# The copy of x in 5 KB pieces, a new order for TensorE, and one row multiplication moved on VectorE

## The chip, the cores and the metric

The kernel runs on one core of a Trainium2 chip. The metric is the time of one execution on the device, in microseconds, as the median of several runs. The core has five engines that this kernel drives, each with its own list of instructions: TensorE (PE; its weight loads are shown apart as PEld), VectorE (DVE), ScalarE (ACT), GpSimd (POOL) and SyncE (SP), which here only issues DMAs. ScalarE and GpSimd issue some DMAs too. Sixteen DMA engines carry the transfers.

## The reference

The input x has 2048 rows of 640 values in bf16; the weights are bf16 too. The output is the input plus two branches that read the same layer-normalised rows.

```python
xn = layernorm(x)                              # over 640, eps 1e-5, no gain and no bias
q  = (xn @ wq) -> 32 heads of 20               # k = xn @ wk, v = xn @ wv: one head, shared
p  = softmax(q k^T * 20**-0.5)                 # 32 x 2048 x 2048
A  = concat(p @ v) @ wo                        # 640 x 640
h  = relu(xn @ w1 + b1)                        # 640 x 1536
B  = (h * h) @ w2 + b2
out = x + A + B
```

## The kernel before, in words

**Tiles.** The 32 heads are taken in 8 groups of 4, the 2048 queries in 4 chunks of 512, which makes 32 blocks. Each block runs over 16 key tiles of 128 keys. So a unit of work (block, key tile) is four score tiles, one for each head, of 128 keys by 512 queries. Unit u stands for block u // 16 and key tile u % 16; score tile t belongs to unit t // 4. A score tile is one matmul with 20 rows of contraction into one of eight PSUM banks.

**Two ways to the exponential.** The score tiles are shared out between two engines. ScalarE takes pairs of tiles with its exponential (line 1083; 693 instructions). VectorE takes single tiles or pairs with a trick of its own (line 1093; 656 instructions): a multiply and an add that write 16-bit integers, whose bits are then read as a bf16 power of two. To make that accurate, four versions of the result with shifted exponents are summed; they are called terms 0 to 3. Terms 1 to 3 are made from term 0 by integer additions, on GpSimd (line 1106, and line 1112 for two at a time) or on VectorE (line 1107). To save matmuls, two terms of a unit are often added into one. Such a pair sum is an accumulating DMA that GpSimd issues (line 1130) or an addition on VectorE (line 1128). The terms live in 15 buffers of 128x2048 called tx. TensorE then multiplies the exponentials by v (widened by a column of ones, which gives the softmax sums), into a PSUM bank for each block.

**The written-out order.** Nothing is scheduled at run time and there is no planner in the file: ORDER gives each engine a list of words (lines 67 to 382), and each engine works through its list in order. Which operation needs which others follows from the code; every such dependence on another engine becomes a semaphore wait. TENANTS (line 383) lists who uses each tx buffer in turn. HELD (line 414) makes each of GpSimd's locked operations wait for a named operation of VectorE. The words that matter here:

- `q:40,41@5,6` are the score matmuls of tiles 40 and 41 for ScalarE, into banks 5 and 6; `a:40` is ScalarE's exponential on them. `d:429.1@5` is the score matmul of head 1 of unit 429 for VectorE, and `e:429.1` its VectorE instruction.
- `p:`, `j:` make shifted terms; `s:`, `b:` are pair sums. `u:429.1` are the four matmuls with v of term 1 of unit 429, which may hold a pair sum; `v:422` those of a unit of ScalarE.
- `T13`, `Q1`, `KT6`, `V1`, `FFN1`, `FFN2`, `FP`, `OUT`, `OF` are TensorE's other work: transposes of xn, the projections q, k, v, the feed-forward and the output projection.
- `CM0_2` is a row multiplication on VectorE (line 976): 128 rows of unnormalised head outputs times the broadcast reciprocals of their softmax sums, for query chunk 0 and column block 2. Its inputs come back through DRAM: the sums are stored (SM), laid out for a reciprocal (SL, RC), stored (RS), and broadcast by DMAs on SyncE's queue (OM, BC). Eight of GpSimd's copies (`p:124.3` is the first) are held on CM0_2.

**The start.** The loads of x, `X0` to `X12`, and the weights go mostly over SyncE's queue, in this order: `X0 X2 wq0 X4 X6 X8 b2 X12 xb b1 w11 wq w10 w20`. Some are held by name until an early operation is done (HOLD, line 60). Layer normalisation of row tile st is a statistics step (bn_stats), a reciprocal root `PW` on GpSimd (line 676) and the scaling `XN` on VectorE or GpSimd (line 677); then TensorE transposes (`T`, line 700), and projects. GpSimd's list at the start ends `... PW10 XN10 PW11 XN11 PW12 XA PW13 PW14 XN14 PW15 XN15 LIB` before its first copies.

**The tensor xb.** For the residual the kernel wants x + b2 in row order. xb is a tensor in DRAM of the same size as x, 2048x640 in bf16, 2560 KB. `xb` on SyncE's queue copies x there, DRAM to DRAM (line 647). `XA` on GpSimd's queue is a DMA that adds the broadcast b2 to it in place (line 648); it waits for the copy and for the load of b2. Later, loads `XR` (line 869) fetch 128 rows at a time for the last step of each row tile. `wd0` to `wd3` (lines 641 to 644) are other copies from DRAM to DRAM, of parts of wo. TensorE's list near the arrival of wq is `q:38,39@3,4 q:40,41@5,6 Q1@2 Q1 T12@1 Q1 T13@0 q:42,43@3,4 Q1`; Q1 is the first use of the big load wq.

Of the kernel before, what the change touches and what calls it, by code (L numbers as in the profile page):

```python
# [38 lines left out]
def _pl(z):  # L39
# [455 lines left out]
def bass_parallel_sum__grouped_kv_mqa__dense_activation_squared_relu__prompt_kernel(nc, A_x, A_wq, A_wk, A_wv, A_wo, B_x, B_w1, B_b1, B_w2, B_b2, out):  # L495
    es = ExitStack()
    with es:
# [98 lines left out]
        def load(name, eng, fn, deps=()):  # L596
            return op(name, eng, fn, deps, dma=one())
# [723 lines left out]
```

## Time and profile before

| | |
|---|---|
| median of 3 runs | 663.84 us (662.64 to 665.05) |
| the profiled execution, its own time | 664.51 us |
| its span | 662.7 us |
| mean granted TensorE clock | 1.000 |
| PE / PEld busy | 654.4 / 216.9 us |
| DVE busy | 625.3 us |
| ACT busy | 649.7 us |
| POOL busy | 536.7 us |

The span runs from the first to the last instruction of the profiled execution, and the time lies 1.8 us above it. Busy times are sums of instruction durations on an engine. TensorE's 99% needs care: its matmuls are pipelined and their ends are modelled, so that a TensorE that is kept waiting in short pieces still looks busy; the waits of its weight loads tell more. In a row of the timeline the first number is the start, the second the duration, and the brackets hold the idle time before it and what ended it.

### The profile page before, as it was taken

Reading aid. Unit: us, or ns where it says so; the run is one execution under the profiler, and the core shown is the slowest. Engines: PE = TensorE matmul, PEld = TensorE weight load, DVE = VectorE, ACT = ScalarE, POOL = GpSimd, SP = SyncE. Lnnn points to the kernel's source line nnn. Section 1 sums busy time; section 2 is a strip of 40 time slices with the busy share of each in tenths; the row PEclk is TensorE's granted clock in tenths of the full one; section 3 lists DMA queues with packets and bytes.
Section 4 is the critical chain, followed back from the end, with each engine's and each line's share of the span. In section 5 each row is a group of like instructions: output and inputs, shape, how many; then the busy total and the mean of one; then the engine's idle time right before and its main releaser. Section 6 shows DMA issues by size and latency. Waiting matters only on the chain.

```text
span 662.7 us, 22005 instructions
## 1 busy us (share of the span) xinstructions
PE 654.4 (99%) x9422; PEld 216.9 (33%) x9422; DVE 625.3 (94%) x1123; ACT 649.7 (98%) x716; POOL 536.7 (81%) x532
## 2 busy tenths in 40 slices
PE   8999999999999999999999999999999999999998
PEld 4432222333322223333332222333333322223444
DVE  8879999999999999999999999999999999999997
ACT  7999999999999999999999999999999999999996
POOL 1729899899898889898999989888999988899400
PEclk9999999999999999999999999999999999999999
DMA  8794857888897995696957645798888654858732
GB/s 293 187 245 96 185 110 163 166 183 187 185 186 161 183 182 120 129 184 125 178 107 155 122 92 99 151 189 170 158 174 165 132 121 91 178 105 177 141 110 71
DMA packets 53814, 102.06 MB, mean 154 GB/s; under 512 B 15948, under 2 KB 31452, under 8 KB 53652
## 3 DMA queue, kind: packets, MB, share of 16 engines
q0 software_dynamic: 18544, 68.17, 55.4%
q1 hardware_dynamic: 34308, 31.94, 16.8%
q8 instruction: 74, 1.21, 0.8%
q10 hardware_dynamic: 864, 0.54, 0.3%
q14 instruction: 24, 0.20, 0.1%
HBM read 23.26 MB, written 10.01 MB: 50 GB/s over the span
## 4 chain that ended last, share of the span: by engine, by line
PE 58%; ACT 34%; DMA 3%; DVE 3%; SPq 1%; issue 0%; POOL 0%
PE ps L600 57%; ACT PT L1083 34%; DVE tx L1093 1%; DMA tx<-tx 1%; DMA cmore<-drs 1%; DMA tx<-in_A_x_dram 1%; PE ps L1005 1%; SPq L800 0%; SPq L969 0%; SPq L963 0%; DVE xnT L694 0%; SPq L622 0%; DVE OR L662 0%; PE ps L700 0%; PE ps L703 0%
## 5 line engine op out<-in xcount | busy, mean ns | idle before, releaser
L1083 ACT ACTIVATE PT<-ps 128x1024 bf16<-128x1024 f32 (+1 forms) x693 | 640.4, 1089 | 2.3 <-PE ps L600 1.9
L1093 DVE TENSOR_SCALAR tx<-ps 128x512 uint16<-128x512 f32 x656 | 424.8, 683 | 21.8 <-PE ps L600 15.1
L1106 POOL INT64_ADD tx<-tx x375 | 396.3, 1132 | 54.3 <-DVE big L836 15.2
L600 PE MATMUL ps<-qT,kT 20*128 20x512 bf16 x2048 | 265.4, 384 | 3.3 <-ACT PT L1083 1.2
L600 PEld LDWEIGHTS ps<-qT,kT 20*128 20x128 bf16 x2048 | 69.0, 91 | 248.7 <-ACT PT L1083 132.4
L600 PE MATMUL ps<-PT,vx 128*32 128x512 bf16 x1392 | 131.7, 383 | 0.0
L1130 POOL DMA_DIRECT2D tx<-tx x118 | 121.3, 1028 | 10.3 <-POOL tx L1106 7.8
L600 PE MATMUL ps<-tx,vxs 128*32 128x512 bf16 x1220 | 115.4, 384 | 0.0
L600 PE MATMUL ps<-tx,vx 128*32 128x512 bf16 x864 | 81.3, 384 | 0.5 <-DMA tx<-tx 0.5
L600 PE MATMUL ps<-w_sb,big 128*32 128x320 bf16 x1536 | 79.1, 302 | 0.0
L600 PE MATMUL ps<-xnT,w_sb 128*32 128x512 bf16 x960 | 78.0, 383 | 0.0
L1107 DVE TENSOR_SCALAR tx<-tx 128x2048 uint16<-128x2048 uint16 x89 | 61.2, 700 | 0.6 <-PE ps L600 0.2
L600 PEld LDWEIGHTS ps<-PT,vx 128*32 128x32 bf16 x1392 | 34.6, 95 | 39.1 <-issue 31.1
L600 PEld LDWEIGHTS ps<-w_sb,big 128*32 128x32 bf16 x1536 | 33.8, 95 | 30.2 <-issue 20.0
L600 PEld LDWEIGHTS ps<-tx,vxs 128*32 128x32 bf16 x1220 | 30.0, 94 | 36.1 <-issue 27.1
L828 DVE TENSOR_SCALAR hT_tmp<-ps,b1col 128x512 bf16<-128x512 f32 x48 | 35.7, 744 | 0.8 <-PE ps L600 0.6
L600 PE MATMUL ps<-xnT,wq_sb 128*32 128x512 bf16 (+2 forms) x480 | 35.5, 357 | 0.0
L600 PEld LDWEIGHTS ps<-tx,vx 128*32 128x32 bf16 x864 | 21.4, 94 | 26.2 <-issue 21.5
L600 PEld LDWEIGHTS ps<-xnT,w_sb 128*32 128x32 bf16 x960 | 19.9, 95 | 28.8 <-issue 19.3
L600 PE MATMUL ps<-wo_c,OC 128*32 128x320 bf16 x496 | 28.0, 301 | 0.0
L1112 POOL INT64_ADD tx<-tx x14 | 26.9, 1924 | 0.9 <-DVE big L836 0.5
L944 DVE COPY OR<-ps 128x512 f32<-128x512 f32 x30 | 20.4, 680 | 1.7 <-PE ps L600 1.6
(87 smaller groups left out, 221.5 us busy)
## 6 DMA issues: line engine op xcount, KB each, us to landing
tx<-tx POOLq DMA_DIRECT2D x111, 512.0 KB, 5.9
tx<-tx POOLq DMA_DIRECT2D x7, 1024.0 KB, 8.8
w_sb<-in_B_w_dram SPq DMA_DIRECT2D x8, 480.0 KB, 9.6
big<-OR SPq DMA_DIRECT2D x71, 40.0 KB
xb<-in_A_x_dram SPq DMA_DIRECT2D x1, 2560.0 KB, 11.1
xb<-b2r POOLq DMA_DIRECT2D x1, 2560.0 KB, 19.8
xr<-xb SPq DMA_DIRECT2D x16, 160.0 KB, 3.2
out_dram<-out_sb SPq DMA_DIRECT2D x14, 160.0 KB, 3.6
```

Source lines behind the costliest of these rows:

```text
L600: return lambda e: e.matmul(out_(), l, val(r), start=val(start), stop=val(stop), tile_position=tp, skip_group_check=loose)
L828: o = evac(ref, f"RL{qc}_{f}", "DVE", lambda e: e.tensor_scalar(out=hT_tmp[:, k % 2, :], in0=ps[:, ref.n, :], scalar1=b1col[:, f:f + 1], s ...
L944: tn = evac(pv_ref[b], f"TN{b}", "DVE", lambda e: e.tensor_copy(out=OR[:, a, :], in_=acc()), or_users[a])
L1005: parts = [lambda e, l=l, r=r, first=first, last=last: e.matmul(ps[:, at(ref), 0:HW], l, r, start=first, stop=last, skip_group_check=k < N ...
L1083: o = op(f"a:{a}", e, lambda e, qk=qk, slots=slots: e.activation(out=some(PT, slots), in_=some(ps, [r.n for r in qk.takes]), func=AF.Exp, ...
L1093: o = op(f"e:{a}", e, lambda e, x=x, i=i, n=n, refs=refs: e.tensor_scalar(out=x.ref(0)[:, i * 512:(i + n) * 512].bitcast(U16) if n == 1 el ...
L1106: fn = dict(POOL=lambda e, x=x, j=j: e.int64_add(out=x.ref(j).bitcast(I64), in0=x.ref(0).bitcast(I64), in1=TSTEP * j * 0x0001000100010001) ...
L1107: DVE=lambda e, x=x, j=j: e.tensor_scalar(out=x.ref(j).bitcast(U16), in0=x.ref(0).bitcast(U16), scalar1=TSTEP * j, scalar2=None, op0=ALU.a ...
L1112: o = op(f"j:{w}", e, lambda e, x=x: e.int64_add(out=two(*sorted((x.at[2], x.at[3]))).bitcast(I64), in0=two(*sorted((x.at[0], x.at[1]))).b ...
L1130: fn = (lambda e, x=x: e.dma_start(*reversed(sums_of(x.at)), accum_op=ALU.add)) if k == "b" else (lambda e, x=x, p=pairs[0]: e.dma_start(x ...
```

## The change

There are three edits.

First, the copy of x to xb. Before, both sides were read as 128 places of 16 rows each (20 KB in one piece), which is contiguous over the whole tensor. Now the 16 rows of each place are cut into four pieces of 4 rows (5 KB), and the pattern goes over the four pieces outermost, then over the 128 places. The same bytes go to the same addresses.

Second, TensorE's list is written anew. It holds the same 3,184 words. 1,146 of them stand at another position, by at most 27 entries; the first difference is entry 260. 247 of the bank numbers differ. Among the words that move are 18 uses of pair sums (`u:429.1`, `u:95.1`, `u:124.3` and others), which stand later.

Third, in VectorE's list CM0_2 moves behind four other entries. The lists of ScalarE, GpSimd and SyncE, TENANTS and HELD are as before.

```diff
 # TensorE's list, near 160 us
-        "q:468,469@0,1 d:143.2@5 u:125.3 v:112 u:127.2 q:470,471@2,3 d:142.0@5 d:143.3@6 d:142.2@4 q:472,473@0,1 u:124.3 u:126.3 u:124.2 d:142.1@5 q:474,475@2,3 v:116 q:476,477@0,1 "
+        "d:143.1@6 u:126.2 d:143.2@5 d:123.3@4 q:468,469@0,1 u:125.3 v:112 u:126.3 u:127.2 q:470,471@2,3 d:142.0@6 u:127.1 q:472,473@0,1 d:142.2@4 d:143.3@5 u:125.2 v:116 q:474,475@2,3 "
...
 # TensorE's list, near 546 us
-        "u:429.3 q:1690,1691@0,1 d:446.1@5 u:428.1 u:429.1 d:446.2@6 q:1692,1693@2,3 v:421 v:419 u:428.2 d:445.1@5 q:1694,1695@0,1 d:445.0@4 u:427.3 u:426.3 u:426.0 q:1696,1697@2,3 "
+        "u:429.3 u:427.3 u:426.0 q:1692,1693@2,3 d:446.2@5 v:421 d:445.0@6 q:1694,1695@0,1 d:445.1@4 u:426.3 u:428.1 d:446.3@5 q:1696,1697@2,3 u:429.1 v:422 FFN2_3@4 d:444.0@6 "
...
 # VectorE's list
-        "e:126.3 e:126.1 p:127.2@8 e:125.3 e:125.0 e:124.2@13 e:125.1 QCe1_1 p:125.1@7 e:124.0 e:124.1 p:126.3@0 e:123.0@4 TN6 FE29 e:123.1 e:124.3 CM0_2 e:143.0@1 e:123.2 FE30 e:143.1 "
+        "e:126.3 e:126.1 p:127.2@8 e:125.3 e:125.0 e:124.2@13 e:125.1 QCe1_1 p:125.1@7 e:124.0 e:124.1 p:126.3@0 e:123.0@4 TN6 FE29 e:123.1 e:124.3 e:143.0@1 e:123.2 FE30 e:143.1 CM0_2 "
...
-        l_xb = load("xb", "SP", lambda e: e.dma_start(xb.rearrange("(p a) d -> p (a d)", p=128), A_x[0].rearrange("(p a) d -> p (a d)", p=128)), [HOLD["wq"]])
+        l_xb = load("xb", "SP", lambda e: e.dma_start(xb.rearrange("(p g a) d -> g p (a d)", p=128, g=4), A_x[0].rearrange("(p g a) d -> g p (a d)", p=128, g=4)), [HOLD["wq"]])
```

305 rows, old and new, of the table ORDER are left out of this document.

## The prediction, made before the result was known

> **What bounds the kernel now.** I read the page's busy shares first, then the costliest group of ScalarE, then the list of waits (total us, count, us each).
>
> ```profile
> span 662.7 us, 22005 instructions
> PE 654.4 (99%) x9422; PEld 216.9 (33%) x9422; DVE 625.3 (94%) x1123; ACT 649.7 (98%) x716; POOL 536.7 (81%) x532
> ...
> L1083 ACT ACTIVATE PT<-ps 128x1024 bf16<-128x1024 f32 (+1 forms) x693 | 640.4, 1089 | 2.3 <-PE ps L600 1.9
> ```
>
> ```profile
> PEld ps L600 <- ACT PT L1083: 134.5, 355, 0.7
> ...
> DVE OC L976 <- DMA cmore<-drs: 1.1, 1, 1.1
> ...
> PEld ps L600 <- DMA tx<-tx: 0.8, 1, 0.8
> ```
>
> PE's 99% is no work bound: 355 times its weight loads waited for ScalarE to give back a score bank. ScalarE is the bound. Its 693 exponentials fill 640.4 us and it idled 2.3 us before them; neither their number nor their order changes. So the time is the start, 640 us of exponentials, the exponentials' idle time, and a tail. An idle microsecond of ScalarE is a microsecond of the kernel, and no later work gives it back. ScalarE's timeline after the first 29 us shows where such idle time is (start, length, and in brackets the idle time before it):
>
> ```profile
> 29.39 131.64 ACT L1083 ACTIVATE PT<-ps 128x1024 bf16<-128x1024 f32 x143
> 161.23 9.28 ACT L1083 ACTIVATE PT<-ps 128x1024 bf16<-128x1024 f32 x10 [0.20 <-PE ps L600]
> 171.29 329.50 ACT L1083 ACTIVATE PT<-ps 128x1024 bf16<-128x1024 f32 x358 [0.79 <-PE ps L600]
> 500.98 45.94 ACT L1083 ACTIVATE PT<-ps 128x1024 bf16<-128x1024 f32 x50 [0.19 <-PE ps L600]
> 547.18 69.36 ACT L1083 ACTIVATE PT<-ps 128x1024 bf16<-128x1024 f32 x75 [0.26 <-PE ps L600]
> 616.72 37.72 ACT L1083 ACTIVATE PT<-ps 128x1024 bf16<-128x1024 f32 x41 [0.18 <-PE ps L600]
> ```
>
> **The change, part one: what the new orders can win.** The five gaps sum to 0.20+0.79+0.19+0.26+0.18 = 1.62 us; that is all that a better order of PE or VectorE can take from idle time of this size. Two have a cause that the change touches. The 0.26 us at 547 follow PE's 0.8 us wait for a pair sum (its DMA, tx<-tx), which the list of waits shows once; the new order takes u:429.1 twelve entries later. The 0.79 us at 171 follow VectorE's wait for a broadcast row:
>
> ```profile
> 166.15 1.30 DVE L1093 TENSOR_SCALAR tx<-ps 128x512 uint16<-128x512 f32 x2
> 168.51 0.69 DVE L976 TENSOR_TENSOR OC<-cmore 128x512 bf16<-128x512 f32 x1 [1.05 <-DMA cmore<-drs]
> 169.12 1.28 DVE L1093 TENSOR_SCALAR tx<-ps 128x512 uint16<-128x512 f32 x2
> 170.32 0.48 DVE L890 TENSOR_TENSOR OC<-ps,xr 128x320 f32<-128x320 f32 x1
> ```
>
> ```profile
> 169.39 3.06 POOL L1106 INT64_ADD tx<-tx  x3 [1.90 <-PE ps L600]
> ```
>
> The multiplication at 168.51 is CM0_2. It moves behind three of the 0.6 us instructions (two start in 1.28 us) and the 0.48 us one, so it would start near 167.4+3×0.6+0.45 = 169.7, a microsecond after its row landed. The wait goes. What is late next is GpSimd: eight of its copies are held on CM0_2 by name, the first three being the x3 at 169.39, which start 0.2 us after CM0_2 ends. They would start near 170.5, 1.1 us later. That delay is hidden only if the pair sums behind these copies have as much to spare; if not, PE pays up to 1.1 us there. The rest of PE's order (1,146 of 3,184 entries at other places, by at most 27, the first near 67 us) keeps the same matmuls, and its switches between score groups and other work go from 1,302 to 1,300, so its work costs nothing more. A nearby reordering can also make gaps like the 0.2 us ones. Bounds: 1.6 us won, 1.1 us lost. I take 0.8 us won: both named gaps (1.05 us) less a little for GpSimd.
>
> **Part two: the copy of x.** Its pattern was 16 rows for each of 128 places, contiguous over the whole tensor. Now its outermost count is g = 4, then 128, then 5 KB. What this does to the spread over the DMA engines is the question. [...]
>
> ```profile
> xb<-in_A_x_dram SPq DMA_DIRECT2D x1, 2560.0 KB, 11.1
> xb<-b2r POOLq DMA_DIRECT2D x1, 2560.0 KB, 19.8
> ...
> tx<-in_A_x_dram SPq DMA_DIRECT2D x2, 160.0 KB, 3.1
> ...
> wod<-in_A_wo_dram SPq DMA_DIRECT2D x1, 120.0 KB, 2.4
> ...
> wod<-in_A_wo_dram SPq DMA_DIRECT2D x1, 100.0 KB
> ...
> wod<-in_A_wo_dram SPq DMA_DIRECT2D x1, 60.0 KB
> ```
>
> The three last go from DRAM to DRAM on SyncE's queue, as the copy does. The one with 96 outer rows has a landing time; the two whose outermost count is 4 (4×20 rows and 4×12 rows, the same form as 4×128 pieces) have none. [...] I take it that each outer row goes to one engine, which is four engines; the other end is sixteen, as now. [...]
>
> How fast one engine goes follows from two stretches inside the copy (the last two columns are the mean busy share of 16 engines and GB/s):
>
> ```profile
> 11.00:12.00 1.00, 1.00 (x47) 0.74 (x47) 1.00 (x5) 1.00 (x3) 0.00 (x0) 1.00 1.76 586
> 13.00:14.00 1.00, 0.57 (x7) 0.24 (x6) 1.00 (x5) 0.74 (x2) 0.53 (x1) 1.00 1.55 614
> ```
>
> 614/(1.55×16) = 24.8 GB/s, and 586/(1.76×16) = 20.8 GB/s, for each busy engine. Four engines carry 2,621,440/4 = 655,360 bytes each: 26.4 us at 24.8, 31.5 us at 20.8. The fixed part of a transfer is about 2.7 us (the 160 KB load: 3.1 us less 10 KB/24.8). So landing takes 29.1 to 34.2 us in place of 11.1. I take 29.1, for four engines are less crowded than sixteen. Issuing 512 pieces costs SyncE what a 640-piece load costs, 0.64 us against 0.50, which nobody waits for. Who waits for the landing:
>
> ```profile
> 9.80 0.50 SPq L647 DMA_DIRECT2D xb<-in_A_x_dram  x1
> ...
> 19.09 0.60 SPq L630 DMA_DIRECT2D w_sb<-in_B_w_dram  x1
> ...
> 19.73 0.64 SPq L628 DMA_DIRECT2D wq_sb<-in_A_wq_dram  x1
> ...
> 25.96 1.82 POOL L648 DMA_DIRECT2D xb<-b2r  x1
> 27.99 0.56 POOL L676 TENSOR_TENSOR rstd<-mv,nhalf 128x1 f32<-128x1 f32 x1 [0.21 <-DVE mv L667]
> ...
> 29.00 0.75 DVE L677 TENSOR_SCALAR big<-tx,mv,rstd 128x640 bf16<-128x640 bf16 x2
> 29.29 0.61 PE L600 MATMUL ps<-xnT,wq_sb 128*20 128x512 bf16 x8
> ...
> 30.56 0.47 PE L700 MATMUL ps<-ident,big 128*128 128x128 bf16 x5
> ```
>
> The copy is issued at 9.80 and landed at 20.9; with four engines it lands at 38.9 (44.0 at the slower rate). First gate: GpSimd's accumulating DMA XA (25.96) waits for it, and GpSimd works in order, so queued behind it are PW13, PW14, XN14, PW15 and XN15, and behind those VectorE's XN13 and PE's T13 (30.56). From XA to T13 the least is 1.82+0.21+0.56, then half of the 0.75 us pair and two releases, about 3.4 us: T13 at 42.3, 11.7 us late. Second gate: wq (19.73) and the w1 load ahead of it (19.09) are queued behind the copy on SyncE's queue:
>
> ```profile
> w_sb<-in_B_w_dram SPq DMA_DIRECT2D x2, 480.0 KB, 5.9
> wq_sb<-in_A_wq_dram SPq DMA_DIRECT2D x1, 700.0 KB, 5.7
> ```
>
> If each engine takes them in order, the four busy ones have still 480/16 = 30 KB and 700/16 = 44 KB to move, 3 us at 24.8 GB/s: wq at 41.9, where Q1 on PE needs it at 29.29, 12.6 us late. Either gate stops PE, whose order puts every further score group behind Q1 and T13. The shift is the later of the two, not their sum; I take 12.2 us, between them. Bounds: 11 us below, 17 us above (44.0+3 for wq). Cover is missing: from 29.39 ScalarE runs without a gap, so it holds no stock of scores and loses the same 12 us.
>
> After an idle stretch PE may also be slow. Two rows of the same shape, early in the kernel and at its very start (busy us, mean ns of one, idle before):
>
> ```profile
> L1041 PE MATMUL ps<-hT_tmp,OR 128*128 128x512 bf16 x15 | 5.2, 508 | 0.0
> ...
> L710 PE MATMUL ps<-hT_tmp,OR 128*128 128x512 bf16 x3 | 1.5, 626 | 1.3 <-DVE PT L608 1.3
> ```
>
> The page's row of the granted clock has 9 in all slices:
>
> ```profile
> PEclk9999999999999999999999999999999999999999
> ```
>
> The slow matmuls stand at the very start, and whether a pause in mid-kernel would bring them back no row here shows; the sum has none. [...]
>
> The copy's other followers are covered: XA's own 19.8 us would end at 38.9+19.8 = 58.7, and its first reader starts at 53.0 now, which moves to 65.
>
> ```profile
> L869 SPq DMA_DIRECT2D xr<-xb x16: 328/478/1443, 53.0 to 527.5; - x16
> ```
>
> **Sum.** 12.2 - 0.8 = 11.4 us. On the profiled execution (664.51 us, span 662.7 and 1.8 us around it) that is 675.9; this execution lies 0.67 us above the median of the runs, 663.84. Forecast: 675.3.
>
> **Rivals.** *The copy stays hidden.* Its price is 0 if it lands by XA's 25.96, that is within 16.2 us of issue. At 24.8 GB/s that takes 8 engines or more (320 KB each, 13.2+2.7 = 15.9 us). It would be so if the pieces were spread, or joined again to the whole contiguous tensor, in which case the edit does nothing. For it: all pieces together are contiguous, as now. Against it: the blank rows with outer count 4. Then only 0.8 us is left: 663.84-0.8 = 663.0, no change that can be measured; with all 1.62 us and the small gaps won, 661.5, faster.
>
> *GpSimd late behind CM0_2, and no copy trouble*: the 1.1 us of its held copies reach PE, and the reordering makes one or two new gaps of the 0.8 us kind: 663.84+1.1+1.0 = 665.9, barely slower. For it: the 1.90 us idle before 169.39 ended with CM0_2. Against: 1.1 us is all it can be.
>
> *Only one gate, or a half one*: wq overtakes the copy on the twelve free engines and the four others finish early, so that only XA's chain counts and part of it is caught up because GpSimd's normalisations run back to back: 669 to 672. For it: of the 0.75 us pairs that VectorE does between those steps some could run ahead of the landing. Against: T13 alone is enough for 11 us.
>
> **How the numbers follow.** Four engines, both gates or the later one: 0.72, 671 to 683. Half gate: 0.09. Hidden copy: 0.16, of which 0.05 faster and 0.11 within. GpSimd late: 0.03, slower by a hair in half of it. A measurement of this kernel can tell about 0.3%, 2 us, from no change. So slower 0.82, same 0.13, faster 0.05. The likeliest case has 671 to 683 as its own range, worked from 11 and 17 us and the clock's unknown; to hold eight in ten I go down to the half gate's 668 and up to 683.
>
> **What would show it.** The copy's landing near 29 us instead of 11.1, or none printed; packets of 5 KB; XA near 39; a hole of ScalarE from about 31 to 43 us; and after it the same 640 us of exponentials, without the gaps at 171 and 547. A landing time near 11 us for the copy would make the prediction wrong at its root; a late landing with no hole in ScalarE would make it wrong at the gates.

## The result: 681.27 us, and the profile after

The changed kernel takes 681.27 us (median of 5 runs, 679.44 to 681.83), the kernel before beside it 663.99 us (662.64 to 665.05). The ratio is 1.0255, with a 95% interval of 1.0235 to 1.0276: slower by 17.3 us. The profiled execution took 681.83 us with a span of 680.0 us. Medians of the same kernel before in later comparisons were 663.4 to 664.2 us; each experiment is held against the one it ran beside. Single executions of one kernel can be some us longer at a lower granted clock: of 23 of the kernel before, 18 have a clock of 1.000 and take 662.3 to 664.2 us, and five have 0.992 to 0.997 and take 664.6 to 668.9 us.

From the page after, the busy shares, the granted clock, the chain that ended last and ScalarE's group (line numbers are one lower than before):

```profile
PE 659.6 (97%) x9422; PEld 217.7 (32%) x9422; DVE 626.9 (92%) x1123; ACT 650.4 (96%) x716; POOL 535.8 (79%) x532
...
PEclk9959999999999999999999999999999999999999
...
PE ps L599 64%; ACT PT L1082 26%; DMA xb<-in_A_x_dram 4%; PE ps L1004 1%; DVE tx L1092 1%; POOL tx L1105 0%; PE ps L699 0%; DVE tx L1106 0%; POOL xb L647 0%; ACT xnT L695 0%; DVE OR L661 0%; DVE tx L1127 0%; DVE OR L662 0%; DVE ident L612 0%; DVE PT L610 0%
...
L1082 ACT ACTIVATE PT<-ps 128x1024 bf16<-128x1024 f32 (+1 forms) x693 | 641.1, 1086 | 18.6 <-PE ps L599 18.2
```

The busy time of the exponentials is 641.1 us against 640.4, but the idle time ahead of them went from 2.3 to 18.6 us. These 16.3 us and the 0.7 us are 17.0 of the 17.3 us by which the spans differ. The copy of x now stands in the chain with 4% of the span, some 27 us; before it was not in it. And the granted clock has a slice of 5 tenths. ScalarE's timeline shows where the idle time is:

```profile
14.39 17.44 ACT L1082 ACTIVATE PT<-ps 128x1024 bf16<-128x1024 f32 x17 [0.27 <-PE ps L599]
44.68 2.10 ACT L1082 ACTIVATE PT<-ps 128x1024 bf16<-128x1024 f32 x2 [12.84 <-PE ps L599]
47.90 1.02 ACT L1082 ACTIVATE PT<-ps 128x1024 bf16<-128x1024 f32 x1 [1.11 <-PE ps L599]
49.41 1.94 ACT L1082 ACTIVATE PT<-ps 128x1024 bf16<-128x1024 f32 x2 [0.49 <-PE ps L599]
51.70 1.94 ACT L1082 ACTIVATE PT<-ps 128x1024 bf16<-128x1024 f32 x2 [0.35 <-PE ps L599]
54.61 121.48 ACT L1082 ACTIVATE PT<-ps 128x1024 bf16<-128x1024 f32 x132 [0.98 <-PE ps L599]
...
192.02 5.61 ACT L1082 ACTIVATE PT<-ps 128x1024 bf16<-128x1024 f32 x6 [0.41 <-PE ps L599]
198.20 1.02 ACT L1082 ACTIVATE PT<-ps 128x1024 bf16<-128x1024 f32 x1 [0.57 <-PE ps L599]
199.82 319.11 ACT L1082 ACTIVATE PT<-ps 128x1024 bf16<-128x1024 f32 x347 [0.60 <-PE ps L599]
```

There are three things to explain: a hole of 12.84 us from 31.8 to 44.7 us, four gaps of together 2.93 us right behind it, and three gaps of 1.58 us at 192 to 200 us. The hole first, on the engines that the prediction named (SyncE, GpSimd, TensorE), and the DMA view's rows for the big transfers:

```profile
9.77 0.73 SPq L646 DMA_DIRECT2D xb<-in_A_x_dram  x1
16.57 5.43 SPq L630 DMA_DIRECT2D b1row<-in_B_b_dram  x1
...
22.71 7.00 SPq L627 DMA_DIRECT2D wq_sb<-in_A_wq_dram  x1
...
38.02 1.82 POOL L647 DMA_DIRECT2D xb<-b2r  x1 [11.54 <-DMA xb<-in_A_x_dram]
...
41.20 1.04 PE L599 MATMUL ps<-xnT,wq_sb 128*20 128x512 bf16 x8 [11.34 <-DVE mv L669]
```

```profile
xb<-in_A_x_dram SPq DMA_DIRECT2D x1, 2560.0 KB
...
wq_sb<-in_A_wq_dram SPq DMA_DIRECT2D x1, 700.0 KB, 18.4
```

The copy no longer has a landing time, like the outer-count-4 copies before. GpSimd waited 11.54 us for it and issued XA at 38.02, so it landed about 28.2 us after its issue at 9.77. The load wq, issued at 22.71, took 18.4 us in place of 5.7 and landed at 41.1; TensorE's first use of it, Q1, starts at 41.20 after 11.34 us of idling. (The row names a VectorE instruction as the releaser; an experiment below, where that one is early, names the load.) Behind the hole TensorE is slow. From its stretches (us, then busy time of PE, PEld, DVE, ACT, POOL, then the granted clock):

```profile
28.00:30.00 2.00, 1.86 (x48) 0.89 (x36) 1.83 (x8) 2.00 (x4) 0.00 (x0) 1.00 0.26 108
30.00:34.00 4.00, 0.00 (x0) 0.00 (x0) 0.00 (x0) 1.83 (x2) 0.00 (x0) 0.88 0.73 241
34.00:38.00 4.00, 0.00 (x0) 0.00 (x0) 0.00 (x0) 0.00 (x0) 0.00 (x0) 0.50 0.58 191
...
50.00:52.00 2.00, 2.00 (x26) 0.81 (x27) 0.98 (x2) 1.65 (x3) 0.00 (x0) 0.50 1.06 222
...
53.00:54.00 1.00, 1.00 (x28) 0.69 (x24) 0.56 (x3) 0.64 (x1) 0.00 (x0) 0.75 1.10 243
```

The clock fell to a half at about 33.0 us (0.88 over 30 to 34 is 0.96 us at a half), 3.2 us after TensorE's last matmul at 29.9, and came back at about 53.5 us.

### The profile page after: what moved, and what is told of

It is laid out like the page before. It is cut to its first block, busy times and chain, and to the rows that moved or that the text cites. A ratio compares the mean times of both kernels' runs of the same rounds, so it can differ in the third digit from the quotient of the medians.

```text
span 680.0 us, 22015 instructions
## 1 busy us (share of the span) xinstructions
PE 659.6 (97%) x9422; PEld 217.7 (32%) x9422; DVE 626.9 (92%) x1123; ACT 650.4 (96%) x716; POOL 535.8 (79%) x532
## 3 DMA queue, kind: packets, MB, share of 16 engines
q1 hardware_dynamic: 34744, 31.94, 16.3%
## 4 chain that ended last, share of the span: by engine, by line
PE 66%; ACT 26%; DMA 4%; DVE 2%; POOL 1%; issue 0%
PE ps L599 64%; ACT PT L1082 26%; DMA xb<-in_A_x_dram 4%; PE ps L1004 1%; DVE tx L1092 1%; POOL tx L1105 0%; PE ps L699 0%; DVE tx L1106 0%; POOL xb L647 0%; ACT xnT L695 0%; DVE OR L661 0%; DVE tx L1127 0%; DVE OR L662 0%; DVE ident L612 0%; DVE PT L610 0%
## 5 line engine op out<-in xcount | busy, mean ns | idle before, releaser
L1082 ACT ACTIVATE PT<-ps 128x1024 bf16<-128x1024 f32 (+1 forms) x693 | 641.1, 1086 | 18.6 <-PE ps L599 18.2
L599 PE MATMUL ps<-tx,vxs 128*32 128x512 bf16 x1220 | 113.1, 384 | 1.1 <-POOL tx L1105 1.1
L1106 DVE TENSOR_SCALAR tx<-tx 128x2048 uint16<-128x2048 uint16 x89 | 63.1, 721 | 0.3
L599 PE MATMUL ps<-xnT,wq_sb 128*32 128x512 bf16 (+2 forms) x480 | 35.9, 368 | 11.9 <-DVE mv L669 11.3
L599 PEld LDWEIGHTS ps<-w_sb,big 128*32 128x32 bf16 x1536 | 33.8, 95 | 30.3 <-issue 20.4
L599 PEld LDWEIGHTS ps<-tx,vx 128*32 128x32 bf16 x864 | 21.4, 95 | 25.3 <-issue 21.1
L943 DVE COPY OR<-ps 128x512 f32<-128x512 f32 x30 | 20.5, 682 | 2.1 <-PE ps L599 1.9
```

The lines of the kernel that those rows point to most:

```text
L599: return lambda e: e.matmul(out_(), l, val(r), start=val(start), stop=val(stop), tile_position=tp, skip_group_check=loose)
L943: tn = evac(pv_ref[b], f"TN{b}", "DVE", lambda e: e.tensor_copy(out=OR[:, a, :], in_=acc()), or_users[a])
L1082: o = op(f"a:{a}", e, lambda e, qk=qk, slots=slots: e.activation(out=some(PT, slots), in_=some(ps, [r.n for r in qk.takes]), func=AF.Exp, ...
L1106: DVE=lambda e, x=x, j=j: e.tensor_scalar(out=x.ref(j).bitcast(U16), in0=x.ref(0).bitcast(U16), scalar1=TSTEP * j, scalar2=None, op0=ALU.a ...
```

## The experiments

**The parts, each alone.** The copy alone; both orders with the old copy; CM0_2 alone; TensorE's order alone.

```diff
 a1_copy_only: the kernel before, with
-xb.rearrange("(p a) d -> p (a d)", p=128)            # and the same for x
+xb.rearrange("(p g a) d -> g p (a d)", p=128, g=4)
 a2_orders_only: the changed kernel, with these two lines the other way
 a3_row_mult_only: the kernel before, with
-e:123.1 e:124.3 CM0_2 e:143.0@1 e:123.2 FE30 e:143.1
+e:123.1 e:124.3 e:143.0@1 e:123.2 FE30 e:143.1 CM0_2
 a4_tensore_only: the kernel before, with the new list of TensorE
```

> The kernel before with only the new pattern of the copy of x. My theory: the whole loss is the late landing of the copy. The trace after shows ScalarE idle for 12.84 us at 31.8 and for 1.11, 0.49, 0.35 and 0.98 us up to 54.6, in all 15.8 us; all of these should be here, and the copy should land about 28 us after its issue at 9.8. Time 663.99+15.8 = 679.8 us (678.5 to 681.3). Rival: the new orders share in the loss (the gaps of 1.58 us at 192 to 200 in the trace after are theirs, and perhaps some of those at the start); then this kernel keeps below 678.5.

> The changed kernel with the old pattern of the copy, so only the new orders of TensorE and VectorE. By the prediction: both named gaps (0.79 and 0.26 us) are gone and nothing is lost, 663.99-0.8 = 663.2 us. Rival, GpSimd late behind CM0_2: its held copies start late, TensorE waits for terms (0.38 and 0.67 us as in the trace after), ScalarE gets gaps of 0.41, 0.57 and 0.60 us near 176 to 184; then 663.99-1.05+1.58 = 664.5 us. No hole at the start by either.

> The kernel before with only CM0_2 moved behind four entries on VectorE. By the prediction VectorE's wait of 1.05 us and ScalarE's gap of 0.79 us go, and GpSimd's eight held copies start about 1.1 us later without harm: 663.2 us. Rival: the late copies reach TensorE as waits for terms made by GpSimd, 0.4 to 0.7 us each, and the time is 664 to 665 us.

> The kernel before with only TensorE's new order. By the prediction the gap of 0.26 us at 547 goes with the wait for the pair sum, the gap of 0.79 us at 171 stays: 663.7 us. Rival: the new order makes new gaps of the 0.2 us kind, as many as it takes: 664.0 us, and with a loss of its own near 180 us, 665 us.

| kernel | us, median | beside the kernel before |
|---|---|---|
| copy alone | 678.79 (678.09 to 680.48) | 663.53, ratio 1.0233 (1.0211 to 1.0256) |
| both orders | 665.11 | ratio 1.0030 (1.0004 to 1.0056) |
| CM0_2 alone | 669.31 (665.8 in two runs, 669.3 to 671.7 in four) | ratio 1.0077 (1.0047 to 1.0107) |
| TensorE's order alone | 663.36 | ratio 1.0009 (0.9982 to 1.0035) |

The copy makes 678.79-663.53 = 15.3 us and the orders 665.11-663.53 = 1.6 us, together 16.8 of the 17.3. With the copy alone, ScalarE's gaps behind 31 us are these:

```profile
44.59 2.10 ACT L1083 ACTIVATE PT<-ps 128x1024 bf16<-128x1024 f32 x2 [13.23 <-PE ps L600]
47.81 1.02 ACT L1083 ACTIVATE PT<-ps 128x1024 bf16<-128x1024 f32 x1 [1.12 <-PE ps L600]
49.32 3.93 ACT L1083 ACTIVATE PT<-ps 128x1024 bf16<-128x1024 f32 x4 [0.49 <-PE ps L600]
53.47 123.14 ACT L1083 ACTIVATE PT<-ps 128x1024 bf16<-128x1024 f32 x134 [0.22 <-PE ps L600]
176.80 338.46 ACT L1083 ACTIVATE PT<-ps 128x1024 bf16<-128x1024 f32 x368 [0.20 <-PE ps L600]
515.45 114.91 ACT L1083 ACTIVATE PT<-ps 128x1024 bf16<-128x1024 f32 x125 [0.19 <-PE ps L600]
```

Its time lies in the range of my theory (678.5 to 681.3), 1 us below its middle; but that the copy is the whole loss does not hold, for the orders cost 1.6 us beside it. Something unforeseen is in the last two rows. After 176.80 there is no gap like the 0.79 us of before, though CM0_2 stands at its old place. And the 125 exponentials from 515.45 run through the place of the 0.26 us gap (547 us before), though TensorE's list is the old one. VectorE's rows of that multiplication, with the old place of CM0_2, in four kernels (copy alone, TensorE's order alone, and the two copies of the next set, which change nothing at this place):

```profile
182.95 0.68 DVE L976 TENSOR_TENSOR OC<-cmore 128x512 bf16<-128x512 f32 x1
```

```profile
167.31 0.68 DVE L975 TENSOR_TENSOR OC<-cmore 128x512 bf16<-128x512 f32 x1
```

```profile
169.36 0.69 DVE L976 TENSOR_TENSOR OC<-cmore 128x512 bf16<-128x512 f32 x1 [1.27 <-DMA cmore<-drs]
```

```profile
167.51 0.69 DVE L976 TENSOR_TENSOR OC<-cmore 128x512 bf16<-128x512 f32 x1 [0.43 <-DMA cmore<-drs]
```

The wait for the broadcast row was 1.05 us in the execution that I read, and 0, 0, 1.27 and 0.43 us in these. ScalarE's gap behind it was 0.79 us there, and none, none, 1.01 and 0.17 us here, so it follows the wait. Each kernel was profiled once, so that the wait varies between executions of one kernel is inferred from five kernels that do the same at this place; the 0.79 us were no fixed gain in any case, and neither were the 0.26. What the move costs is seen better. With CM0_2 alone moved, GpSimd, TensorE and ScalarE show:

```profile
175.54 3.05 POOL L1106 INT64_ADD tx<-tx  x3 [3.39 <-DVE OC L976]
...
178.65 0.40 PE L600 MATMUL ps<-tx,vxs 128*32 128x512 bf16 x4 [1.02 <-POOL tx L1106]
...
179.45 7.44 ACT L1083 ACTIVATE PT<-ps 128x1024 bf16<-128x1024 f32 x8 [1.24 <-PE ps L600]
```

GpSimd idles 3.39 us for CM0_2 (1.90 before, and 0.75 with the copy alone, where the row was there in time), TensorE then waits 1.02 us for a term that GpSimd made, and ScalarE loses 1.24 us. So the rival, GpSimd late, holds, and it costs more than I gave it: 2.3 us by the two runs at 665.8 (against 663.53), of which ScalarE's rows show 1.24 us here and 0.33 us at 187. The four other runs have a further loss, and a granted clock of 0.987 to 0.995 where the two have 1.000. In the profiled one of them (669.33 us) the granted clock's row has a slice of 7 tenths, from 16.7 to 33.4 us, its mean of 0.995 over the 667.5 us of the span makes some 6.7 us at a half, and ScalarE has three gaps of 1.92, 0.20 and 1.42 us between 14 and 24 us; without these 3.54 us it would be 665.8 too. Why so many of this kernel's runs have it stays open; two runs of the kernel before, of 23, were as long (668.48 and 668.87). TensorE's new order by itself changes nothing that can be measured; together with the move it takes back some 0.7 us of the 2.3 (by the two runs at 665.8). The rest is the gaps of 0.41, 0.57 and 0.60 us in the changed kernel; with both orders and the old copy the same three are there, 0.40, 0.57 and 0.60 us. Both waits for GpSimd's terms stand in the trace after:

```profile
188.15 3.05 POOL L1105 INT64_ADD tx<-tx  x3 [3.37 <-DVE OC L975]
...
191.26 0.40 PE L599 MATMUL ps<-tx,vxs 128*32 128x512 bf16 x4 [0.38 <-POOL tx L1105]
...
197.08 0.40 PE L599 MATMUL ps<-tx,vxs 128*32 128x512 bf16 x4 [0.67 <-POOL tx L1105]
```

**The same pieces, larger counts.** The pieces stay 512 of 5 KB; only the outermost count of the pattern changes.

```diff
 the kernel before, with
-xb.rearrange("(p a) d -> p (a d)", p=128)            # and the same for x
+xb.rearrange("(p g a) d -> g p (a d)", p=64, g=8)    # b1_outer8
+xb.rearrange("(p g a) d -> g p (a d)", p=32, g=16)   # b2_outer16
```

> The kernel before with the copy in the same 5 KB pieces, but with 8 as the outermost count and 64 places. My theory: each outer row goes to one DMA engine, so 8 engines carry 320 KB each, 13.2 us at 24.8 GB/s and 2.7 us around it: landing about 16 us after issue, near GpSimd's 25.96, and wq a little late behind it. Loss 0 to 2 us, 664 to 666. Rival: 5 KB pieces themselves are slow and the count of engines does not matter: landing near 28 us and about 680 us.

> The kernel before with the copy in the same 5 KB pieces, but with 16 as the outermost count and 32 places. My theory: 16 engines carry it, it lands within 11 to 12 us as before, and the time is 664.0 us (663 to 665). Rival: small pieces from DRAM to DRAM are slow by themselves: landing near 28 us and about 680 us.

The first took 664.66 us, the second 663.72, the kernel before beside them 664.15; neither is apart from it (the ratio's interval is 0.9948 to 1.0024 and 0.9938 to 1.0025). With 8, GpSimd's row says when the copy had landed, and TensorE's next row what was left of the second gate; with 16 the DMA view has a landing time again:

```profile
26.90 1.82 POOL L648 DMA_DIRECT2D xb<-b2r  x1 [1.50 <-DMA xb<-in_A_x_dram]
...
29.92 0.61 PE L600 MATMUL ps<-xnT,wq_sb 128*20 128x512 bf16 x8 [1.14 <-DVE mv L667]
```

```profile
xb<-in_A_x_dram SPq DMA_DIRECT2D x1, 2560.0 KB, 11.9
```

Landing takes 28.2 us with 4, 26.90-9.77 = 17.1 us with 8, and 11.9 us with 16. The rival that pieces of 5 KB are slow by themselves is dead. I had assumed that each outer row goes to one DMA engine. By it 4 and 8 engines with 26.4 and 13.2 us of bytes at 24.8 GB/s differ by 13.2 us, and measured they differ by 11.1. With 16 the same sum would be 6.6+2.7 = 9.3 us; 11.9 are measured, near the 11.1 of the old pattern, so with 16 the rate that was read for four is not kept. The traces' records of single packets show it: the copy's 512 packets of 5 KB were on the mean 3.9 at a time under way with a count of 4, 7.5 with 8 and 12.9 with 16, each at 25.5, 24.3 and 20.1 GB/s. (The old pattern went as 64 packets of 40 KB, 14.5 at a time, each at 21.4 GB/s.) The traces' landing records go the same way: the copy before has sixteen, the changed kernel's copy has five, one at 10.90 us and four at 37.06 to 37.70, and of the sixteen of wq behind it twelve stand at 33.1 to 33.8 us and four at 40.4 to 41.1. That fits a copy that kept four of sixteen engines busy; no record names an engine.

**The two gates apart.** The copy keeps its outer count of 4. XA goes behind the normalisations on GpSimd, or wq goes ahead of the copy on SyncE's queue, or both.

```diff
 a1_copy_only, with
-PW12 XA PW13 PW14 XN14 PW15 XN15 LIB       # GpSimd
+PW12 PW13 PW14 XN14 PW15 XN15 XA LIB       # c1_add_late, c3_both
+PW12 PW13 PW14 XN14 PW15 XN15 LIB XA       # c5_both_lib_first
-X12 xb b1 w11 wq w10                       # SyncE
+X12 wq xb b1 w11 w10                       # c2_wq_ahead, c3_both, c5_both_lib_first
```

> Only the new copy, and GpSimd's accumulating DMA XA moved behind XN15, so that no normalisation waits for the copy. If XA on GpSimd is the gate, the hole goes: 664 to 667 us. If wq, queued behind the copy, is the gate, the hole of 12.8 us stays whole, since Q1 waits until 41.1: 679 to 680 us. Both gates are within 0.2 us of each other in the trace after (XA's chain lets T13 go near 41.2, wq lands near 41.1), so I expect the second.

> Only the new copy, and the load wq issued ahead of it on SyncE's queue. If wq is the only gate, the hole goes: 664 to 667 us. If XA on GpSimd is a gate of its own, T13 waits until about 42 and the hole stays: 679 to 681 us, which I expect.

> Only the new copy, with both moves: XA behind XN15 on GpSimd, and wq ahead of the copy on SyncE's queue. By the theory of two gates the hole goes, although the copy still lands near 38 us and XA near 57 us: 664 to 666 us. If something else waits for the copy (b1 behind it on the queue, the loads XR from 53 us on), a hole of 2 us or more stays.

With XA late the time is 680.62 us, with wq ahead 678.80; each gate alone keeps the whole hole (12.47 and 13.66 us of ScalarE, against 13.23 with the copy alone). TensorE's rows at the end of the hole, first with XA late, then with wq ahead:

```profile
41.37 1.03 PE L600 MATMUL ps<-xnT,wq_sb 128*20 128x512 bf16 x8 [10.97 <-DMA wq_sb<-in_A_wq_dram]
```

```profile
40.20 1.82 POOL L648 DMA_DIRECT2D xb<-b2r  x1 [14.73 <-DMA xb<-in_A_x_dram]
...
43.18 0.73 PE L700 MATMUL ps<-ident,big 128*128 128x128 bf16 x5 [13.05 <-DVE mv L667]
```

In the first the load itself is named: TensorE idles 10.97 us for wq. In the second wq is long there (it landed 4.9 us after its issue), and TensorE waits 13.05 us for the transpose's normalised rows, 3 us behind XA. With both moved, the hole of 31 to 45 us is gone, as expected, but the time is 677.55 us (673.23 to 688.78) where 664 to 666 were expected: a new wait came, which I had not foreseen. From GpSimd, TensorE and ScalarE of that kernel:

```profile
40.27 1.82 POOL L648 DMA_DIRECT2D xb<-b2r  x1 [7.13 <-DMA xb<-in_A_x_dram]
51.50 4.08 POOL L1106 INT64_ADD tx<-tx  x4 [9.41 <-issue]
...
53.60 0.62 PE L600 MATMUL ps<-tx,vxs 128*32 128x512 bf16 x4 [4.47 <-POOL tx L1106]
...
14.12 36.07 ACT L1083 ACTIVATE PT<-ps 128x1024 bf16<-128x1024 f32 x37 [0.65 <-PE ps L600]
55.26 1.02 ACT L1083 ACTIVATE PT<-ps 128x1024 bf16<-128x1024 f32 x1 [5.07 <-PE ps L600]
```

ScalarE runs 36 us through the place of the hole. But XA stood ahead of GpSimd's library load LIB. Its 9.41 us began only after XA, the first copies came at 51.50, and TensorE ran out of terms. From 50.9 to 85.0 us the granted clock stood at a half, and in that stretch ScalarE has 17 more gaps, 10.4 us together. So the move was made once more, with XA behind LIB.

> As the kernel with both moves, but XA now stands behind LIB, GpSimd's library load, whose 9.41 us without an instruction were what delayed the first copies there (51.50 after XA at 40.27). With wq ahead of the copy and XA behind LIB, the copy may land near 40 us and nobody should wait for it but XA: GpSimd's first copy starts near 42, no hole of ScalarE at 31 to 45, no lowered clock, 664 us (663.3 to 666). If a third follower of the copy exists, a gap of more than 1 us stays and names it.

```profile
11.60 43.57 ACT L1083 ACTIVATE PT<-ps 128x2048 bf16<-128x2048 f32 x44
58.43 1.02 ACT L1083 ACTIVATE PT<-ps 128x1024 bf16<-128x1024 f32 x1 [3.26 <-PE ps L600]
...
41.80 1.81 POOL L648 DMA_DIRECT2D xb<-b2r  x1 [9.40 <-issue]
...
57.73 0.61 PE L600 MATMUL ps<-qT,kT 20*128 20x512 bf16 x4 [3.41 <-DMA qT<-QCr]
```

The 44 exponentials from 11.60 to 55.17 have no gap, with the copy's count still 4: the two gates are all that the hole was made of. The time is not settled by that. The 12 runs lie between 664.88 us (granted clock 1.000) and 687.63 us, with a median of 673.63, where 663.3 to 666 were expected. The profile shown is of one of the three longest (685.66 us, clock 0.968), and in it a third follower appears: TensorE waits 3.41 us for a small load of the projected queries (qT<-QCr), while XA's 2560 KB and the weights that came late are under way. That these crowd the small load out was not tried. In the execution shown the clock then stood at a half from about 57.2 to 101.6 us (0.86 over 50 to 60, 0.50 from 60 to 100, 0.92 over 100 to 110). What the other runs lose no profile shows.

**The clock.** TensorE is kept busy through its wait by matmuls on zeros.

```diff
 a1_copy_only, with
-q:40,41@5,6 Q1@2 Q1 T12@1
+q:40,41@5,6 fill ... fill Q1@2 Q1 T12@1    # 26 fills in c4_fill, 53 in c6_fill_full
```

> Only the new copy, with 26 groups of matmuls on zeros put on TensorE ahead of Q1, which add nothing to the result and keep TensorE busy for about 10 of the 11.3 us that it waits. By the theory that a lowered clock makes the gaps of 1.11, 0.49, 0.35 and 0.98 us after the hole, the granted clock stays at 1.00, these gaps go, and the time is 2.9 us (2 to 3.3) below the kernel with the new copy alone, near 677 us. Rival: the gaps come from late work on GpSimd and VectorE, and stay: 680 us.

> Only the new copy, with 53 groups of matmuls on zeros ahead of Q1 (26 of them took 5.79 us and left TensorE idle for 6.76 us, and the clock still fell to a half at 39.7). 53 take 11.8 us, so TensorE is hardly idle. By the theory that the lowered clock makes the gaps behind the hole (1.12, 0.49 and 0.22 us with the copy alone), the clock stays at 1.00 and the time is 1.8 us lower than with the copy alone: near 677.0 us. Rival: the gaps are late work of other engines and stay: 678.8 us. The hole itself, about 13 us, stays by both.

The 26 groups of four took only 5.79 us: the row holds 104 matmuls that overlap, for one on zeros is listed with 389 ns in the trace before. TensorE still idled 6.76 us, the clock fell to a half (0.87 over 38 to 40 us, 0.50 from 40 to 48), and the time was 679.24 us: nothing was won, and the test said nothing. With 53 the clock stays up and the time is 674.96 us (674.49 to 675.43), 3.8 us below the copy alone. From its page and ScalarE's timeline:

```profile
PEclk9999999999999999999999999999999999999999
```

```profile
44.09 129.64 ACT L1083 ACTIVATE PT<-ps 128x1024 bf16<-128x1024 f32 x141 [12.87 <-PE ps L600]
```

The hole is there (12.87 us), and the gaps behind it are not: 141 exponentials run through. So the gaps were the clock's, not late work of other engines. The saving is twice the 1.8 us that I had read off the listed gaps. The two profiled executions differ by less than the medians, 678.09-675.43 = 2.7 us, of which 1.8 us are the gaps and 0.4 us the hole (13.23 to 12.87). The other 0.5 us, and the 1.1 us by which the medians differ more, no row shows.

## Why the prediction was right, and where it was not

The forecast was 675.3 us, in a range of 668 to 683; measured are 681.27. The direction and the cause were right, and the loss was 17.3 us where 11.4 were forecast. The bounds of the two terms alone (17 us lost, 0.8 won) would end at 680.0 us; it is the allowance for the clock's unknown in the range that takes in 681.27.

*The bound.* Right: the exponentials' 641.1 us and the tail stayed, and the whole loss is ScalarE's idle time (16.3 us of it in the group's row).

*Four engines.* Right, as far as the records tell. The blank landing times of the outer-count-4 copies were the sign (in the trace before, each of the two has five landing records and the one of 96 rows has sixteen), and with counts of 4, 8 and 16 the copy landed 28.2, 17.1 and 11.9 us after its issue. Landing 28.2 us, 29.1 were forecast. That each outer row goes to one engine was an assumption; no run shows an engine by name, and what the traces show in its place is 3.9 packets under way at a time with a count of 4. The rate held as well: a packet went at 25.5 GB/s with a count of 4, where 24.8 were taken, and at 20.1 with 16: with fewer under way each was faster. The shares of 1.76 and 1.55 from which it was read are above 1, so they are sums over packets and not counts of busy engines; what they give is the rate of a packet.

*Two gates, the later one counts.* Right in place, size and in that they do not add: Q1 at 41.20 (41.9 forecast), XA at 38.02 (38.9 forecast), each gate alone keeps the hole. Without the clock's share the copy costs 674.96-663.37 = 11.6 us, where the step said 12.2.

*The clock, "the sum has none".* This term was mis-sized. It was left at zero because no row of before showed a pause in mid-kernel; the run with 53 fills shows 3.8 us by the medians, and the changed kernel's own gaps behind the hole are 2.93 us. The allowance for the clock in the range was an estimate of mine that no run shows. In its place the changed kernel showed a fall 3.2 us after TensorE's last matmul and a return that took from 41.20 to 53.5 us, 12.3 us of a TensorE that its rows show busy.

*The new orders, "0.8 us won".* This step failed, in sign. They cost 1.6 us (the interval of the ratio is 0.3 to 3.7 us), where at most 1.1 were to be lost. Two things were wrong in it. The 0.79 us at 171 were read from one execution; the wait ahead of it, 1.05 us there, was 0, 0, 0.43 and 1.27 us in four others. The 0.26 us at 547 were gone in the copy alone too, without the new order. And "They would start near 170.5, 1.1 us later" took the late row for granted. Without it CM0_2 could start at once, and the same move delays GpSimd's eight held copies by more: GpSimd idles 3.4 us where it idled 1.9 with the late row and 0.75 without it, and TensorE waits for its terms. The fate that I gave the delay ("hidden only if the pair sums behind these copies have as much to spare") was asked and then answered without a row: they had not as much.

*The sum.* With the measured terms it is 11.6+3.8+1.6 = 17.0 us against 17.3. The last 0.3 us are not assigned. Two small slips are in the forecast's own sums: 675.9 less 0.67 is 675.2 and not 675.3, and 44.0+3 for wq, less 29.29, is a bound of 17.7 us and not 17.

*The rivals.* Hidden copy: no, with 4; but it is what happens with 16, and nearly with 8, as its price said (15.9 us forecast for 8, 17.1 measured; ScalarE's gap at that place is 1.27 us). GpSimd late: it came on top, not instead. Half gate: no, wq did not overtake the copy (it landed at 41.1 us, XA followed the copy at 38.02), and either gate alone keeps the hole.

## What to carry to other kernels

Before a DMA's pattern is rewritten, look at its outermost count: here 4, 8 and 16 had 3.9, 7.5 and 12.9 packets under way at a time, and 4 in place of 16 made a copy of 2560 KB land 28.2 us after its issue instead of 11.9, with the load wq behind it on the queue late as well (18.4 us in place of 5.7). A pause of TensorE can cost more than its length, because the half clock behind it makes the bounding engine wait on: 3.8 us here, by the kernels with the copy alone and with 53 fills. In these profiles the pauses of 3.41 us (XA behind LIB), 4.47 (both moves), 6.76 (26 fills), 11.34 (the changed kernel) and 11.73 us (the copy alone) were each followed by the half clock; those of 1.02 us (CM0_2 alone, at 178 us), 1.14 (a count of 8) and 1.18 us (53 fills) were not. A wait that one trace shows on a DMA's landing may be absent in the next; price the removal by several profiles, and look first at who is held by name on the instruction that is to move.

## What the runs showed that I had not expected

SyncE's issue of later loads stalled behind the slow copy: the 3 KB load of b1 took 5.43 us to issue and wq 7.00 us, where before they took 0.40 and 0.64 us. So the loads were late in being issued, not only in being carried out.

The clock's return differs widely. After the pause it came back 12.3 us after TensorE's work had begun again in the changed kernel, and in the kernel with both moves it was at a half from about 51 to 85 us, 31 us after work began at 53.60, with TensorE's rows full all the time:

```profile
60.00:70.00 10.00, 10.00 (x79) 1.62 (x71) 5.28 (x8) 6.63 (x7) 4.34 (x5) 0.50 0.21 55
...
84.00:86.00 2.00, 2.00 (x23) 0.33 (x15) 1.25 (x3) 1.50 (x2) 0.82 (x1) 0.74 0.35 72
```

What decides when it returns stays open. In these two kernels a full row of TensorE did not suffice. The stretch at a half lasted 10.2 us with 26 fills, 17.1 with the copy alone, 20.5 in the changed kernel, 34.1 with both moves and 44.4 with XA behind LIB. And the fall came 1.8 us (both moves) to 4.8 us (26 fills) after the last matmul ahead of the pause, so the delay was not the same in each.
